# Chunk 0's logits without paired products, short matmuls on ones, a later last store, and a new order of pieces

## The chip, the cores and the metric

The kernel runs on one core of a Trainium2 chip. The metric is the device time of one execution in microseconds; three runs give a median of 217.93 us (217.93 to 218.11).

## What is computed

A layer norm (without weights) of x [2048 x 640] feeds two branches, and the output is x plus both:

```python
def reference(A_x, A_wqkv, A_wo, B_x, B_w1, B_b1, B_w2, B_b2):
    xn = _layernorm(A_x)
    return A_x + _A_ref(xn, A_wqkv, A_wo) + _B_ref(xn, B_w1, B_b1, B_w2, B_b2)
# _A_ref: q, k, v = xn @ wqkv, 32 heads of 20; position s attends to s, s-2, ..., s-14
#         (8 keys, those before 0 masked); softmax; weighted sum of v; @ wo
# _B_ref: gelu(xn @ w1 + b1) @ w2 + b2, width 1536
```

## The kernel before

The 2048 rows are worked off in four chunks (n = 0 to 3) of 512 rows, each of four blocks of 128 rows. One list, ORDER (L38), names small pieces of work; L703 emits them in that order, and every engine, and the DMA queues of SyncE (SP) and ScalarE (ACT), executes its own instructions in the order of emission. GpSimd (POOL) issues the accumulating stores from its queue. A name is a kind, then the chunk, then block or tile:

- `st`, `su`, `sq`, `rs`, `rc`, `xn`: statistics and layer norm. Chunks 0 and 1 take `st` on VectorE (L203; block 1 of chunk 0 on ScalarE), chunks 2 and 3 take `su` and `sq` on ScalarE. `rs` is a square root on ScalarE, `rc` a reciprocal on VectorE.
- `tp`, `tc`: transposition of xn, through TensorE for chunk 0 (copies on VectorE and ScalarE, L279), by DMA from SP for the others (L286).
- `ga`, `gb`, `gd`, `ge` (L331) and `hj<which><pair><columns>` (L362): q, k, v of chunk 0, of one block or of two blocks at a time; `gc` and `hc` empty their PSUM banks on ScalarE. `pj<n><which><tile>` (L318) and `pc` (L377) do that for chunks 1 to 3, in five matmuls of 512 columns each.
- `qk<n><block><half>` (L402): products of q and shifted k on VectorE, eight a chunk, four window steps by five tiles each. `pa` (L420): adds tile 1 to tile 0 and tile 3 to tile 2 of the products, four instructions a chunk, in the chunks named in PAIRED.
- `lg` (L429): sums the products over a head by matmuls with a matrix of zeros and ones. A matmul for every tile, half and block: 3 x 2 x 4 = 24 where products are paired, 5 x 2 x 4 = 40 where not.
- `m`, `mx`, `ex`, `ss`, `ri`, `at`: softmax, on VectorE but for the exponential `ex` on ScalarE. `xd` (SP) and `xs` (ScalarE's queue) copy the attention weights to all rows of a head (L499). `av` (L514), `ad` (L523), `ot` (L528): weighted sum of v on VectorE; `ot` leaves oT.
- `f1<n>_<ft>` (L535): the hidden layer, five matmuls of 512 columns a piece; `ge` with a chunk and a number (L551): bias and GELU on ScalarE. The piece named only `ge` belongs to q.
- `o<n><block><pc>` (L571 the first 512 columns, "lo"; L573 the last 128, "hi"): the output. Parts 0 to 3 take w2, part 4 takes oT and wo. `oc` (L578, L579) empties lo and hi into osb on ScalarE, `od` (L584) adds osb to the output in memory from POOL's queue. `xp`, `xb`: x and the bias b2 go to the output in memory first.
- The last block, 3,3, has its lo in `o330` to `o334`, its hi in `ohi`; `oclo` and `ochi` add x on VectorE (L592, L601) and store without accumulation, `oclo` from SP (L593), `ochi` from ScalarE's queue (L604).
- `tb` and `b1` (L411, L414): transposition of b1 and its copy on VectorE. `ho` builds the matrix for `lg`.

PSUM: psA has four banks, for q, k, v, hidden pieces, transposes and a part of the last chunk's output; psL holds the logits (and the tiles `idle` and `tb`), psO one lo and one hi. osb has two buffers. `table()` (L164) loads ScalarE's function table when sqrt, exp and GELU alternate. Before the list, ten matmuls on ones (L701) run.

Of the kernel before, what the change touches and what calls it, by code (L numbers as in the profile page):

```python
# [13 lines left out]
BF16 = mybir.dt.bfloat16  # L14
F32 = mybir.dt.float32

S, D, F, H, W, DIL = 2048, 640, 1536, 32, 8, 2
P = 128
# [3 lines left out]
CH = 512  # L22
NCH = S // CH
BPC = CH // P
# [5 lines left out]
LASTB = S // P - 1  # L30
WARM = 10

PAIRED = (0, 2, 3)
ACT_STATS = (2, 3)

COLS = ((0, 2), (2, 4), (4, 5))

ORDER = """  # L38
pad01 pad02 st00a st00 sum1 rs00 mean1 neg1 rc00 sq1 xn00a xn00b tp00a tp00b tc00a rs01 tb ga tc00b rc01 xn01 gb2 b1
tp01 gb3 tc01a tc01b gb4 gd gc0 ge st03a st03 rs03 gc1 hj100 st02a rc03 ho hc100 hj101 st02 rs02 hj201 xn03 tp03 rc02  # L40
xn02 st11a st12a st11 st10a gc4 st13a tp02 hc101 tc03 tc02 hc201 hj102 hj200 hc200 hj011 hc102 st10 hc011 st13 st12
rs1 rc1 qk000 qk001 xn12 tc12 hj112 hc112 xn11 qk011 hj010 hc010 tc11 hj111 hj110 hj202 hc202 hc111 qk010 pa010 hj012
hc012 hc110 qk021 qk030 qk031 xn10 qk020 pa011 hj211 hc211 tc10 hj212 f10_11 f10_2 xn13 tc13 hc212 ge0_2 f10_9 ge0_9
f10_0 ge0_0 f10_6 pj114 ldx ld2 pj100 ge0_6 pc100 pj110 pc110 pj102 pad11 pa000 pj112 pa001 lg0 mask m0 ge0_11 pc114
mx0 pc112 pj111 pc102 su22 su20 ex0 ss0 pj103 pj113 pc103 pc111 pc113 pj104 pc104 pj101 pc101 ri0 at0 f10_1 qk110
qk130 f11_9 qk120 su23 f10_10 qk101 ge1_9 su21 f11_10 ge0_10 ge0_1 ng2 f11_3 ge1_3 sq21 f10_4 ge0_4 sq23 f11_0 ge1_0
pj124 pc124 qk121 sq22 f11_7 ge1_7 f10_7 xd0 qk100 qk131 sq20 pj121 ge0_7 rs2 hj210 hc210 qk111 xs0 lg1 ldo rc2 pc121
xn23 av001 tc23 m1 pj123 pc123 av000 xn22 av010 f10_5 av020 av011 mx1 f11_4 o000 ge0_5 ge1_10 xn21 f10_3 ge0_3 tc22
f10_8 av030 ge0_8 xn20 f11_5 ge1_5 o001 o002 o003 tc21 ex1 pj122 av021 xp0 xb0 ss1 pj120 xp1 pc122 tc20 pj211 pc211
xb1 av031 pc120 su32 ri1 ad00 pj204 pc204 at1 xd1 ad01 ad02 ot0 pj203 pad12 av111 pc203 av101 su30 pj222 pc222 pj224  # L50
pc224 pj221 pc221 xs1 av121 pj212 pc212 pj220 pc220 pj223 pj202 pc202 pc223 pj213 pc213 pad22 su33 pj201 f11_1 pc201
su31 av110 pj210 o004 oc00 od00 pj214 av100 pad21 pc214 pc210 ng3 sq31 av130 o020 o021 av131 av120 o022 o023 sq30 sq32
o024 oc02 sq33 rs3 rc3 pj200 pc200 xn31 tc31 o030 o031 o032 o033 o034 xn30 tc30 oc03 ad10 od03 f11_6 o010 o011 o012
ge1_4 xn32 pad31 ad11 tc32 ad12 o013 qk211 xn33 f12_0 o014 f12_4 ge1_1 ge1_6 oc01 od01 ot1 qk221 ge2_0 qk230 qk231
qk220 qk210 ge2_4 qk201 pa211 pa210 f11_2 ge1_2 tc33 pj320 pj304 pc304 qk200 pa201 pj301 pc301 pj324 pj310 pc324 pa200
pj303 pc303 pj323 pc323 pad32 pc320 pj312 pj302 xp2 pc302 pj314 pc314 pc312 xl pj313 pj300 pc313 pj311 f13_6 lg2 pc311
m2 pc310 ge3_6 o130 pc300 qk310 mx2 f11_8 ge1_8 f12_10 o131 o132 qk321 ex2 ss2 ri2 at2 qk301 qk330 qk320 qk331 qk300
f13_11 pa311 f13_5 ge3_5 f13_10 ge3_10 ge2_10 qk311 ge3_11 f13_4 f13_0 xs2 f13_3 ge3_3 pa300 ge3_4 ge3_0 f11_11 ge1_11
f12_8 f12_9 pa301 ge2_8 f13_8 ge3_8 pj322 o133 o134 oc13 od13 pc322 f13_1 ge3_1 pa310 o110 o111 o112 lg3 m3 xd2 av210
xb2 mx3 f12_3 ge2_3 av211 ex3 ss3 f12_7 f13_2 o113 o114 oc11 od11 od02 f13_7 ge3_7 av200 ri3 o100 av230 o101 o102 o103  # L60
xb3 ge3_2 o104 oc10 at3 xs3 f12_6 av231 o120 f12_2 ge2_2 av201 av221 ge2_9 ge2_7 o121 o122 av220 o123 od10 f12_5 ge2_5
f12_11 o124 oc12 od12 ad20 ad21 ad22 ot2 pj321 pc321 av331 xd3 av300 av301 av321 f12_1 ge2_1 av311 ge2_6 f13_9 o210
ge3_9 o211 ge2_11 o212 o213 o310 o214 oc21 od21 o330 o331 o200 o201 o202 o203 o204 oc20 od20 o311 o312 o220 o221 o222
av330 av310 o223 o224 o313 av320 ad30 oc22 od22 ad31 ad32 o230 o231 o232 o233 o234 oc23 od23 o332 o333 o320 o321 o322
o323 ot3 o324 oc32 od32 o314 o300 o334 o301 o302 o303 o304 ohi oc31 od31 oclo ochi oc30 od30
""".split()


# [1 line left out]
def kernel(  # L70
# [16 lines left out]
    nc = tc.nc  # L87
# [3 lines left out]
    out_sd = out.rearrange("b s d -> (b s) d")  # L91
# [5 lines left out]
    psL = ctx.enter_context(tc.tile_pool(name="psL", bufs=1, space=bass.MemoryType.PSUM))  # L97
# [73 lines left out]
    mask = consts.tile([H, W, MW], BF16, name="mask")  # L171
# [20 lines left out]
    tiles = {}  # L192
# [207 lines left out]
    def do_qk(n, j, h):  # L400
# [5 lines left out]
            op=ALU.mult,  # L406
        )

    def do_tb():
        tiles["tb"] = psL.tile([P, 2 * W * P], BF16, tag="L", name="tb")  # L410
        nc.tensor.transpose(tiles["tb"][:, 0:MW], b1_rt[:], ident[0:MW, 0:MW])  # L411
# [10 lines left out]
    def do_lg(n):  # L422
        L = psL.tile([P, W, P], F32, tag="L", name="L")
        tiles["L", n] = L
        ts = range(0, KT, 2 if n in PAIRED else 1)
        for t in ts:
# [160 lines left out]
    last = (NCH - 1, BPC - 1)  # L587
# [11 lines left out]
    def do_ochi():  # L599
        osb = tiles["osb", last]  # L600
        nc.vector.tensor_tensor(  # L601
            out=osb[:, CH:D], in0=tiles["hi", *last][:, 0 : D - CH], in1=x_sb[:, LASTB, CH:D], op=ALU.add
        )
        nc.scalar.dma_start(out_sd[LASTB * P :, CH:D], osb[:, CH:D])  # L604

    pieces = {}

    def piece(name, fn, *args):
        assert name not in pieces
        pieces[name] = lambda: fn(*args)  # L610

    for name in "tb b1 mean1 ho ldx ld2 ldo xl oclo ohi ochi mask".split():
        piece(name, locals()[f"do_{name}"])
    for u, a, b, eng, own in (("a", 0, 2, "ve", "lo"), ("b", 2, KT, "se", "hi")):
        piece(f"xn00{u}", do_xn, 0, 0, a, b)
# [13 lines left out]
            piece(f"tc0{bl}", do_tc, 0, bl, 0, KT, "se")  # L629
    piece("sum1", do_su, 0, 1)  # L630
    piece("neg1", do_ng, 0, 1, 2)
    piece("sq1", do_sq, 0, 1)
    piece("ga", do_ga, 0, 2)
    for ti in range(2, KT):
# [10 lines left out]
    for n in range(NCH):  # L645
# [23 lines left out]
        for h in range(2):  # L669
            for j in range(BPC):  # L670
                piece(f"qk{n}{j}{h}", do_qk, n, j, h)
                piece(f"av{n}{j}{h}", do_av, n, j, h)
            if n in PAIRED:
                for c in range(2):
# [20 lines left out]
    engines = {getattr(mybir.EngineType, e) for e in ("PE", "DVE", "Activation", "SP")}  # L695
    with tc.manual_schedule(engines=engines):

        ones = nc.const_aps.tensor(1.0, [P, CH], BF16)
        idle = psL.tile([P, W, P], F32, tag="L", name="idle")
        for _ in range(WARM):  # L700
            nc.tensor.matmul(idle[:, 0:BPC, :], lhsT=ones[:, 0:P], rhs=ones, start=True, stop=True)  # L701
        assert sorted(ORDER) == sorted(pieces)
        for name in ORDER:  # L703
            pieces[name]()
# [30 lines left out]
```

## Time and profile before

| | us |
|---|---|
| median of three runs | 217.93 |
| the profiled execution | 219.77 |
| its span, first to last instruction | 217.4 |
| TensorE busy | 206.9 |
| VectorE busy | 179.2 |
| ScalarE busy | 125.4 |

The page gives the busy time of each engine as a share of the span; a matmul's row lasts until its result has drained, so rows overlap, and the pace is read from the distance of starts. The chain of waits goes back from the last instruction to what released it. The timeline gives each group of instructions with its start, the idle time in front of it, and what ended that. Times in it are microseconds from the span's start.

### The profile page before, as it was taken

Reading aid. Unit: us, or ns where it says so; the run is one execution under the profiler, and the core shown is the slowest. Engines: PE = TensorE matmul, PEld = TensorE weight load, DVE = VectorE, ACT = ScalarE, POOL = GpSimd, SP = SyncE. Lnnn points to the kernel's source line nnn. Section 1 sums busy time; section 2 is a strip of 40 time slices with the busy share of each in tenths; the row PEclk is TensorE's granted clock in tenths of the full one; section 3 lists DMA queues with packets and bytes.
Section 4 is the critical chain, followed back from the end, with each engine's and each line's share of the span. In section 5 each row is a group of like instructions: output and inputs, shape, how many; then the busy total and the mean of one; then the engine's idle time right before and its main releaser. Section 6 shows DMA issues by size and latency. Waiting matters only on the chain.

```text
span 217.4 us, 3276 instructions
## 1 busy us (share of the span) xinstructions
PE 206.9 (95%) x1327; PEld 115.0 (53%) x1327; DVE 179.2 (82%) x166; ACT 125.4 (58%) x239; POOL 19.7 (9%) x37
## 2 busy tenths in 40 slices
PE   8999989999999998999999999999999999999970
PEld 2899635444645554555555544454555455555540
DVE  3578896599799999998999979996999999994010
ACT  5468595999989747689854558631844520111210
POOL 2000000000000500111010400000110101111301
PEclk9999999999999999999999999999999999999997
DMA  6991249418275996015521491702039202222232
GB/s 217 390 398 56 59 108 386 175 18 233 44 142 166 205 186 182 4 29 90 92 30 71 150 175 29 191 5 30 0 39 207 28 13 33 30 30 33 31 59 31
DMA packets 24069, 23.89 MB, mean 110 GB/s; under 512 B 9080, under 2 KB 21880, under 8 KB 24056
## 3 DMA queue, kind: packets, MB, share of 16 engines
q1 hardware_dynamic: 17008, 14.68, 23.3%
q0 software_dynamic: 4144, 4.92, 17.0%
q10 hardware_dynamic: 2904, 4.10, 5.9%
q8 instruction: 10, 0.16, 0.3%
q14 instruction: 3, 0.02, 0.0%
HBM read 10.00 MB, written 7.54 MB: 81 GB/s over the span
## 4 chain that ended last, share of the span: by engine, by line
PE 64%; DVE 13%; issue 11%; ACT 3%; DMA 3%; POOL 2%; ACTq 1%; POOLq 0%; SPq 0%
PE hps L535 19%; PE lo L571 17%; PE pps L318 15%; DVE half L514 5%; PE hi L573 4%; PE gps L362 3%; PE L L429 3%; DVE half L402 3%; DMA wq_sb<-in_A_wqkv_dram 3%; POOL out_dram L584 2%; PE gps L331 2%; DVE half L523 1%; DVE L L451 1%; DVE m L445 1%; ACTq L499 1%
## 5 line engine op out<-in xcount | busy, mean ns | idle before, releaser
L535 PE MATMUL hps<-xnT,w_sb 128*128 128x512 bf16 x240 | 55.4, 379 | 1.3 <-ACT hT L551 0.9
L402 DVE TENSOR_TENSOR half<-qT,kT 128x2560 bf16<-128x2560 bf16 x32 | 45.8, 1484 | 0.7 <-ACT kT L372 0.7
L571 PE MATMUL lo<-w_sb,hT 128*128 128x512 bf16 x144 | 41.0, 379 | 0.0
L535 PEld LDWEIGHTS <-w_sb 128*128 128x128 bf16 x240 | 22.9, 98 | 28.6 <-issue 2.5
L578 ACT CAST osb<-lo 128x512 bf16<-128x512 f32 x15 | 8.8, 585 | 42.7 <-issue 24.6
L573 PE MATMUL hi<-w_sb,hT 128*128 128x128 bf16 x144 | 31.5, 219 | 0.0
L551 ACT ACTIVATE hT<-hps,b1T 128x512 bf16<-128x512 f32 x36 | 23.5, 685 | 11.5 <-PE hps L535 11.5
L514 DVE TENSOR_TENSOR half<-vT,ax 128x2560 bf16<-128x2560 bf16 x16 | 23.1, 1478 | 1.2 <-PE L L429 1.2
L571 PEld LDWEIGHTS <-hT 128*128 128x128 bf16 x144 | 14.1, 98 | 17.2 <-issue 0.4
L571 PE MATMUL lo<-wo,oT 128*128 128x512 bf16 x80 | 23.1, 379 | 0.0
L584 POOL DMA_DIRECT2D out_dram<-osb x15 | 13.0, 864 | 110.0 <-ACT osb L579 94.1
L514 DVE TENSOR_TENSOR half<-vT,x_sb 128x2560 bf16<-128x2560 bf16 x16 | 22.6, 1483 | 0.0
L523 DVE TENSOR_TENSOR half<-half,half 128x5120 bf16<-128x5120 bf16 x8 | 22.3, 2813 | 0.1
L318 PE MATMUL pps<-xnT,wq_sb 128*128 128x512 bf16 x75 | 18.3, 379 | 1.0 <-ACT kT L377 1.0
L318 PE MATMUL pps<-xnT,wk_sb 128*128 128x512 bf16 x75 | 18.5, 379 | 0.0
L318 PE MATMUL pps<-xnT,wv_sb 128*128 128x512 bf16 x75 | 18.0, 379 | 0.0
L167 ACT ACT_TABLE_LOAD x13 | 16.7, 1283 | 1.0 <-PEq L719 0.7
L573 PE MATMUL hi<-wo,oT 128*128 128x128 bf16 x80 | 16.9, 219 | 0.0
L573 PEld LDWEIGHTS <-hT 128*128 128x128 bf16 x144 | 14.1, 98 | 1.7
L420 DVE TENSOR_TENSOR half<-half 128x2048 bf16<-128x2048 bf16 x12 | 14.1, 1216 | 0.0
L318 PEld LDWEIGHTS <-wq_sb 128*128 128x128 bf16 x75 | 8.7, 117 | 8.7 <-issue 1.6
L377 ACT CAST kT<-pps 128x512 bf16<-128x512 f32 x15 | 8.4, 590 | 7.7 <-PE pps L318 4.8
(86 smaller groups left out, 265.4 us busy)
## 6 DMA issues: line engine op xcount, KB each, us to landing
w_sb<-in_B_w_dram SPq DMA_DIRECT2D x4, 960.0 KB, 11.3
out_dram<-osb POOLq DMA_DIRECT2D x15, 160.0 KB, 3.4
out_dram<-b2bc POOLq DMA_DIRECT2D x3, 640.0 KB, 7.1
x_sb<-in_A_x_dram SPq DMA_DIRECT2D x1, 1280.0 KB, 7.8
out_dram<-x_sb ACTq DMA_DIRECT2D x1, 1120.0 KB, 4.8
ax<-attn SPq DMA_DIRECT2D x4, 256.0 KB, 4.3
ax<-attn ACTq DMA_DIRECT2D x4, 256.0 KB, 5.2
x_sb<-attn SPq DMA_DIRECT2D x4, 256.0 KB, 4.5
```

The source lines that it names most:

```text
L167: nc.scalar.activation(warm[:], nc.const_aps.tensor(0.0, [P, 1], F32), func)
L318: nc.tensor.matmul(ps[:], lhsT=wqkv_p[which][:, ti, to, :], rhs=xnT[:, ti, :], start=(ti == 0), stop=(ti == KT - 1),)
L402: nc.vector.tensor_tensor(out=half[h][:, :, :, cs], in0=qkv_tile(n, 0)[:, :, cs].unsqueeze(1).to_broadcast([P, W // 2, KT, P]), in1=window ...
L420: nc.vector.tensor_tensor(out=even, in0=even, in1=odd, op=ALU.add)
L514: nc.vector.tensor_tensor(out=half[h][:, :, :, cs], in0=window(qkv_tile(n, 2), h, cs), in1=ax_view(n)[:, j, ws, :].unsqueeze(2).to_broadca ...
L523: nc.vector.tensor_tensor(out=a, in0=a, in1=b, op=ALU.add)
L535: nc.tensor.matmul(ps[:], lhsT=w1_sb[:, ti, ft * P : (ft + 1) * P], rhs=tiles["xnT", n][:, ti, :], start=(ti == 0), stop=(ti == KT - 1),)
L551: nc.scalar.activation(hT, tiles["hps", n, ft][:], ACT.Gelu_apprx_tanh, bias=b1T[:, ft : ft + 1], scale=1.0)
L571: nc.tensor.matmul(lo[:], lhsT=lhs, rhs=rhs[:, 0:CH], start=first, stop=last)
L573: nc.tensor.matmul(hi[:, 0 : D - CH], lhsT=lhs, rhs=rhs[:, CH:D], start=first, stop=last)
L578: nc.scalar.copy(osb[:, 0:CH], tiles["lo", n, bl][:])
L584: nc.gpsimd.dma_start(rows, tiles["osb", n, bl][:], accum_op=ALU.add)
```

## The change

Six things:

1. PAIRED loses chunk 0: its four `pa` pieces (pa000, pa001, pa010, pa011) are gone, and lg0 has 40 matmuls instead of 24.
2. A function do_warm issues matmuls on ones into the tile `idle`. Ten of 512 columns come first, as before, then three of 128 columns.
3. Two pieces of such short matmuls stand in the list: `wa` (one) behind tp00a, `wb` (two) behind tp00b.
4. The last store from ScalarE's queue is a piece of its own, `ochd`, the last in the list.
5. The tile `idle` is made before the list is built.
6. ORDER is new throughout. Each engine has the same pieces but for those above, in another order.

```diff
-PAIRED = (0, 2, 3)
+PAIRED = (2, 3)
 ACT_STATS = (2, 3)
...
 ORDER = """
-pad01 pad02 st00a st00 sum1 rs00 mean1 neg1 rc00 sq1 xn00a xn00b tp00a tp00b tc00a rs01 tb ga tc00b rc01 xn01 gb2 b1
-tp01 gb3 tc01a tc01b gb4 gd gc0 ge st03a st03 rs03 gc1 hj100 st02a rc03 ho hc100 hj101 st02 rs02 hj201 xn03 tp03 rc02
-xn02 st11a st12a st11 st10a gc4 st13a tp02 hc101 tc03 tc02 hc201 hj102 hj200 hc200 hj011 hc102 st10 hc011 st13 st12
-rs1 rc1 qk000 qk001 xn12 tc12 hj112 hc112 xn11 qk011 hj010 hc010 tc11 hj111 hj110 hj202 hc202 hc111 qk010 pa010 hj012
-hc012 hc110 qk021 qk030 qk031 xn10 qk020 pa011 hj211 hc211 tc10 hj212 f10_11 f10_2 xn13 tc13 hc212 ge0_2 f10_9 ge0_9
-f10_0 ge0_0 f10_6 pj114 ldx ld2 pj100 ge0_6 pc100 pj110 pc110 pj102 pad11 pa000 pj112 pa001 lg0 mask m0 ge0_11 pc114
...
-o323 ot3 o324 oc32 od32 o314 o300 o334 o301 o302 o303 o304 ohi oc31 od31 oclo ochi oc30 od30
+pad01 pad02 st00a st00 sum1 rs00 mean1 neg1 rc00 sq1 xn00a xn00b tp00a wa tp00b wb tc00a rs01 ga tc00b rc01 xn01 gb2
+tp01 gb3 tc01a tc01b gb4 gd gc0 ge tb b1 ho hj102 st02a gc1 st03a hc102 gc4 st02 rs02 st03 hj100 rs03 rc02 hc100 rc03
+xn02 xn03 hj101 st12a hc101 st11a st13a hj201 st10a tp02 tc02 tp03 hj200 tc03 st11 hc201 hc200 hj202 hc202 hj012 hj110
+hc110 st12 st13 st10 rs1 hc012 qk001 hj010 hc010 hj111 rc1 xn12 qk000 qk011 qk010 xn11 hj011 hc011 tc12 tc11 hj112
+hc111 hc112 f10_1 ge0_1 qk020 xn13 tc13 qk030 f10_11 qk031 f10_6 ge0_6 xn10 f10_0 ge0_0 pad11 f10_9 hj211 hc211 ge0_9
+f10_2 hj212 qk021 lg0 hc212 ge0_11 tc10 pj103 ge0_2 pc103 mask m0 mx0 ex0 ss0 pj114 pj101 pc101 pj104 pc104 pj111
+pj113 pc114 pj112 pj102 pc111 ri0 ldx ld2 su23 pj100 pc113 pj110 at0 su21 pc112 su20 f11_0 pc102 pc100 pc110 qk110
+qk101 qk130 f11_7 qk111 qk131 qk120 qk100 f10_4 xd0 su22 ng2 ge1_7 sq20 f11_3 ge1_3 ge1_0 f10_5 sq22 qk121 pj122 ge0_5
+sq21 ldo ge0_4 hj210 xp0 xs0 f10_3 ge0_3 pj121 sq23 rs2 rc2 o000 o001 lg1 hc210 av010 av000 m1 xn21 f10_7 tc21 pc122
...
+o002 pj120 av020 av021 ex1 ss1 pc120 xp1 av031 ri1 pj124 pc124 o003 av011 pad21 tc23 pj213 pc213 pc123 pj202 pc202
+pj211 pc211 pj214 pc214 at1 pj222 pad12 ge1_10 pc222 pj204 pj224 pc224 xs1 pj200 ad01 ad00 pc200 pj201 su31 ad02 ot0
...
+o312 o230 o231 o232 o233 o234 o313 av311 av331 av320 av301 ad31 ad30 ad32 oc23 ot3 o320 o321 o322 o323 o324 o314 od21
+oc32 od23 o300 o301 o302 o303 o304 oc31 od32 o333 o334 od31 oc30 od30 oclo ohi ochi ochd
 """.split()
...
+    ones = nc.const_aps.tensor(1.0, [P, CH], BF16)
+    idle = psL.tile([P, W, P], F32, tag="L", name="idle")
+
+    def do_warm(n, cols):
+
+        for _ in range(n):
+            nc.tensor.matmul(
+                idle[:].rearrange("p w c -> p (w c)")[:, 0:cols],
+                lhsT=ones[:, 0:P],
+                rhs=ones[:, 0:cols],
+                start=True,
+                stop=True,
+            )
...
-        nc.scalar.dma_start(out_sd[LASTB * P :, CH:D], osb[:, CH:D])
+
+    def do_ochd():
+        nc.scalar.dma_start(out_sd[LASTB * P :, CH:D], tiles["osb", last][:, CH:D])
...
+    piece("wa", do_warm, 1, P)
+    piece("wb", do_warm, 2, P)
...
-        ones = nc.const_aps.tensor(1.0, [P, CH], BF16)
-        idle = psL.tile([P, W, P], F32, tag="L", name="idle")
-        for _ in range(WARM):
-            nc.tensor.matmul(idle[:, 0:BPC, :], lhsT=ones[:, 0:P], rhs=ones, start=True, stop=True)
+        do_warm(WARM, CH)
+        do_warm(3, P)
```

## The prediction

> **What bounds the kernel now.** I read the page first, then the chain that ended last, then the timeline of each engine at the start, at TensorE's gaps and at the end.
>
> ```profile
> PE 206.9 (95%) x1327; PEld 115.0 (53%) x1327; DVE 179.2 (82%) x166; ACT 125.4 (58%) x239; POOL 19.7 (9%) x37
> ```
>
> TensorE is the bound: its rows leave almost no holes from 5.46 us to its last matmul, which starts at 210.52 and ends at 210.58 at the pace of its neighbours. I call that end E. So the end moves only by TensorE's work, its holes, or what follows E.
>
> The timeline of TensorE shows the holes (columns: start, duration, engine, line, operation; a group's duration includes the drain of its last matmul, so I count starts: 0.216 us for 512 columns):
>
> ```profile
> 24.84 1.24 PE L535 MATMUL hps<-xnT,w_sb 128*128 128x512 bf16 x5
> 26.44 3.61 PE L535 MATMUL hps<-xnT,w_sb 128*128 128x512 bf16 x15 [0.36 <-ACT kT L372]
> 30.91 1.24 PE L535 MATMUL hps<-xnT,w_sb 128*128 128x512 bf16 x5 [0.85 <-ACT hT L551]
> ...
> 37.47 1.48 PE L429 MATMUL L<-half,head_of 128*32 128x512 bf16 x24
> ...
> 42.16 2.55 PE L318 MATMUL pps<-xnT,wq_sb 128*128 128x512 bf16 x10
> ```
>
> Five matmuls from 24.84 should hand over at 25.92, not 26.44: 0.52 us lost. Fifteen from 26.44 end at 29.68, not 30.91: 1.23. Ten from 42.16 end at 44.32; the next row starts at 44.54: 0.22. At 82.79 another 1.13 goes (ten matmuls from 79.50 end at 81.66), behind ScalarE, which spent 79.79 to 82.11 issuing chunk 1's two copies of attention weights. Sum 3.10 us, each time for a PSUM bank that ScalarE had not emptied.
>
> The timeline after E shows the tail:
>
> ```profile
> 210.62 0.29 DVE L601 TENSOR_TENSOR osb<-hi,x_sb 128x128 bf16<-128x128 f32 x1 [2.81 <-PE hi L573]
> 210.94 0.35 ACTq L604 DMA_DIRECT2D out_dram<-osb  x1
> 211.41 0.58 ACT L578 CAST osb<-lo 128x512 bf16<-128x512 f32 x1 [6.70 <-DVE osb L601]
> 211.89 0.27 ACT L579 CAST osb<-hi 128x128 bf16<-128x128 f32 x1
> 212.46 0.86 POOL L584 DMA_DIRECT2D out_dram<-osb  x1 [6.59 <-ACT osb L579]
> ```
>
> The copies of block 3,0 (oc30) stand in ScalarE's queue behind the last store, which waits for VectorE, which waits for E. So an accumulating store that could have left earlier is issued at E+1.88, lands 3.36 us later at 215.82, and the program ends 1.60 us after that: E+6.84.
>
> **The tail, new order.** After o304, TensorE still has o333 (3 matmuls of 512 columns, 0.65), o334 (5, 1.08) and ohi (17 of 128, 17 x 0.056 = 0.95). So o304 ends at E-2.7. ScalarE's queue is then empty: oc30 takes 0.15 + 0.75 and its store is issued 0.30 later (as 212.16 to 212.46), at E-1.5; 3.36 to land: E+1.9. The other end, ochi and ochd: 0.39 from E to the issue as now, 1.47 to land (the 32 KB row's): E+1.9. Nothing is queued behind ochd. osb has two buffers: oc30 needs od32's landing, about 0.15 + 0.75 + 0.30 + 3.4 = 4.6 us after o324, while o304 ends 1.36 + 4.62 = 6.0 after it. oclo needs od31's, 6.1 after o324, and its operand comes at 7.7. Both covered. With 1.60 behind the landing: E+3.5, so **-3.35 us**. Bounds: -2.5 if stores side by side take 1 us longer, -3.7 if they land as the quickest (3.3).
>
> **Logits without additions.** The 16 more matmuls are priced by chunk 1's row, 40 in 2.44 us, against 24 in 1.44: **+1.0** on TensorE. VectorE drops four additions at 1.135 apart, 4.54 us, but they count only if lg0 waits for VectorE. lg0 now needs all eight products.
>
> ```profile
> 32.44 3.49 DVE L420 TENSOR_TENSOR half<-half 128x2048 bf16<-128x2048 bf16 x3
> 39.01 0.29 DVE L440 TENSOR_TENSOR L<-L,mask 32x128 f32<-32x128 f32 x1 [3.08 <-PE L L429]
> ...
> 46.61 11.31 DVE L402 TENSOR_TENSOR half<-qT,kT 128x2560 bf16<-128x2560 bf16 x8
> ```
>
> VectorE was done at 35.92 and waited for TensorE. In the new order five wk/wq pieces of chunk 1 no longer stand before lg0.
>
> **The new order up to lg0.** From the first k piece (11.35, taken as unchanged): 115 matmuls of 256 columns x 0.109 = 12.54, 10 transposes x 0.056, tb 0.1, six hidden pieces x 1.08 = 6.48: lg0 at 31.0. One wait is added: tb moves behind ge, so b1 on VectorE waits until about 11.6 (it ran at 6.80). Behind it stand ho and the statistics of blocks 2 and 3, which now start at 9.59. That puts xn02 near 15.2 and costs TensorE's transposes about 0.2. The eight statistics of chunk 1 then end near 19.7 (18.12 now), the first product ends at 21.1, rc1 takes 0.35, seven products x 1.402 end near 31.3: level with lg0. Banks: ScalarE must load the GELU table (1.28 + 0.20) after hc112 (near 24.6); its next outputs follow at 26.8, 28.2 and 29.7, and f10_9, hj211, f10_2 ask for those banks at 27.4, 28.5, 29.5. Only the last waits, 0.25. So the 0.52 and 1.23 go, 0.45 comes, and lg0 starts near 31.5.
>
> **From lg0 on.** Chunk 1's first product needs pj110, the tenth piece behind lg0: 31.5 + 2.44 + 10.8 + 0.65 to evict = 45.4 (VectorE is free at about 41.6, so it idles 3.8). Eight products end at 56.6; TensorE reaches lg1 after 10.8 + 8 x 1.08 + 1.09 + 1.63 at 56.1, against 57.60: 0.2 lost, since lg1's first matmuls need only the first products. ScalarE reaches chunk 1's copies of attention weights (xs1) only after pc224, when they are long ready; I charge 0.25 for its 2.32 us of issuing instead of 1.13. Chunk 2's rc3 will stall VectorE about 3 us (0.59 now), as its statistics stay behind oc02; it has that to spare. From lg3's end to the last oT VectorE now needs 48.2 us (150.25 to 198.49). With lg3 ending near 149 that gives 197.2, and o324 is reached at E-10.1 = 199.3. Covered by 2 us; beyond that each microsecond moves the end. The other moves hide behind TensorE. TensorE's sum: -3.10 + 1.0 + 0.45 + 0.2 + 0.25 = **-1.2**. Bounds: +1.9 if as much is lost as now besides what I added, -2.1 if none of my new waits comes.
>
> **The short matmuls on ones.**
>
> ```profile
> 0.78 4.43 PE L701 MATMUL idle<-const-bfloat16-1.0 128*128 128x512 bf16 x10 [0.78 <-PEq L719]
> 5.46 0.79 PE L274 MATMUL tp<-ident,xn 128*128 128x128 bf16 x5 [0.26 <-DVE xn L259]
> 6.19 0.19 PE L411 MATMUL tb<-ident,b_rt 16*128 16x16 bf16 x1
> 6.72 1.79 PE L331 MATMUL gps<-xnT,wq_sb 128*128 128x128 bf16 x15 [0.35 <-DMA wq_sb<-in_A_wqkv_dram]
> 8.84 2.67 PE L331 MATMUL gps<-xnT,wq_sb 128*128 128x128 bf16 x35
> ```
>
> Starts are 0.427 us apart in the first row and 0.107 from 6.72 to 9.91, half pace; from 10.01 they are 0.056. Three matmuls (0.32) now follow the ten and end at 5.32, before 5.46; one and two more fall into the holes at 5.65 and 6.05. They delay nothing as long as xn00a and wq land no earlier. If full pace came before 6.72, about 30 matmuls would take 0.056 instead of 0.107: -1.5. Bounds 0 and -1.5; I take 0, since the five fill only 0.6 of the 1.1 us idle between 5.0 and 6.72, and 4.2 us of unbroken warm-up had not raised the pace.
>
> The Trainium skill, "TensorE: Matmul & The Clock Gate", section "What's actually happening", says that the gate watches free-running windows of 3413 ns and opens after a busy one. The pace here changes 3.3 us after 6.72, which agrees. By the rule a window from 6.6 back to 3.2 would be fuller, and the change would gain the 1.5. Its section "Part 4: PE-mode transpose" says that transposes do not count as busy, which speaks against it, since they fill part of that window; no row here shows whether they count.
>
> **Sum.** -3.35 - 1.2 + 0 = -4.6 us (rounded): span 217.4 to 212.8. The profiled execution took 219.77, 2.37 around its span; it becomes 215.2. The median of the runs shown is 217.93, 1.84 below; the same step gives **213.3**.
>
> **Rivals.**
> - *Full pace comes early*: another -1.5, 211.8; with few of the new waits, 211.0. For it: the holes are filled by half. Against: ten warm matmuls did not do it. 0.20.
> - *The bank waits come back* (also: the new order does not do what it should): four banks and a ScalarE full from 45 to 55 speak for it, the spacing above against. -3.35 + 1.0 + 0 to 0.9: 215.6 to 216.5. 0.23.
> - *Slower: VectorE decides in the last chunk.* lg3 comes so late that the last oT holds o324. The price is 1:1 beyond 2 us of delay; the time is above 217.93 once lg3 ends 6.6 us later than 149. VectorE's 3.8 + 3 us of new idling speak for it, its idling anyway in front of lg2 and lg3 (1.9 in front of lg3) against. 10 us late: 221. 0.09.
>
> **Chances.** Forecast, 212.3 to 214.6: 0.48. About 0.2% (0.4 us) is what a measurement can tell from no change. Faster 0.88 (0.48 + 0.20 + most of 0.23, cut for the edge), same 0.03, slower 0.09. Range 211.0 to 216.4.
>
> **What would show it.** oc30's copies before ochi; the last store's issue at E+0.4; lg0's 40 matmuls near 31.5; no holes at 24 to 31 and 82; starts at 0.107 until about 9.9. It is wrong if E is above 211, or if VectorE's last oT ends less than 10.1 us before E.

## The result, and the profile after

| | before | after |
|---|---|---|
| median, 4 runs each, us | 218.02 (217.93 to 218.63) | 215.08 (214.75 to 215.61) |
| ratio after/before | | 0.9865 (95%: 0.9843 to 0.9887) |
| the profiled execution, us | 219.77 | 215.14 |
| its span, us | 217.4 | 212.6 |
| E, the end of the last matmul | 210.58 | 209.25 |
| tail, span less E | 6.84 | 3.38 |

The change makes the kernel faster by 1.35%. Against the forecast: 213.3 was predicted (212.3 to 214.6), 215.08 came, above that band and inside the whole range. The span was predicted at 212.8 and measured at 212.6, and still the time is 1.8 us off; the first experiment explains that. The ratios leave out single disturbed executions; one of g2_paired_later, the profiled one, took 270 us. (In the prediction the start of the last matmul of before should read 210.36, not 210.52; E is right.)

The busy times, from the page of the profile after:

```profile
PE 205.3 (97%) x1327; PEld 114.6 (54%) x1349; DVE 174.2 (82%) x162; ACT 126.3 (59%) x241; POOL 19.8 (9%) x37
```

VectorE lost 5.0 us and four instructions, the additions. TensorE's share looks better, but its busy time counts the slow pace of the start too, so the share alone says little. (The counts of PE and PEld differ because some matmul records are missing; a doubled distance between two starts shows where.)

The timeline of all engines at the end (start, duration, engine, line, operation, in brackets the idle time in front and what ended it):

```profile
206.60 0.58 ACT L592 CAST osb<-lo 128x512 bf16<-128x512 f32 x1 [3.87 <-PE hi L587]
...
207.65 0.86 POOL L598 DMA_DIRECT2D out_dram<-osb  x1 [3.76 <-ACT osb L593]
...
209.12 0.36 SPq L607 DMA_DIRECT2D out_dram<-osb  x1
209.29 0.29 DVE L615 TENSOR_TENSOR osb<-hi,x_sb 128x128 bf16<-128x128 f32 x1 [0.20 <-PE hi L587]
209.61 0.36 ACTq L620 DMA_DIRECT2D out_dram<-osb  x1
```

The tail is what lies between E and the end of the span. The copy of block 3,0 now runs 2.65 us before E (before: 0.83 after it), its store is issued 1.6 us before E, and the last store 0.36 us after E with nothing behind it. All three stores land within 0.55 us of each other: POOL's at 211.03, SP's at 211.37, ScalarE's at 211.58.

TensorE from the k, v pieces of chunk 0 to lg0 (L443):

```profile
21.35 2.37 PE L549 MATMUL hps<-xnT,w_sb 128*128 128x512 bf16 x9
25.07 3.60 PE L549 MATMUL hps<-xnT,w_sb 128*128 128x512 bf16 x15 [1.35 <-ACT kT L372]
28.82 1.25 PE L362 MATMUL gps<-xnT,wv_sb 128*128 128x256 bf16 x10
30.21 1.24 PE L549 MATMUL hps<-xnT,w_sb 128*128 128x512 bf16 x5
...
31.92 2.34 PE L443 MATMUL L<-half,head_of 128*32 128x512 bf16 x40
```

Counted by starts as in the prediction: two pieces (ten matmuls, one record missing) from 21.35 should hand over at 23.51, not 25.07: 1.56 us lost. Fifteen from 25.07 end at 28.31, not 28.82: 0.51. Ten of 256 columns from 28.82 end at 29.91, not 30.21: 0.30. So 2.4 us of holes stand where 0.25 was priced. The largest is ScalarE's doing; its row in the waits of the profile after (engine, tile, line, whom it waited for: us in all, times, longest):

```profile
ACT kT L372 <- DVE half L402: 2.0, 1, 2.0
```

and its timeline:

```profile
24.44 0.86 ACT L372 CAST kT<-gps 128x512 bf16<-128x512 f32 x2 [2.01 <-DVE half L402]
25.31 1.28 ACT L167 ACT_TABLE_LOAD   x1
```

hc111, a copy of k, waits for a product of VectorE. The kernel before had such waits too, 2.0 us in two, and I passed over them. These are its copies of k of blocks 2 and 3 (hc112, hc111, hc110):

```profile
20.28 0.35 ACT L372 CAST kT<-gps 128x256 bf16<-128x256 f32 x1
...
23.66 0.58 ACT L372 CAST kT<-gps 128x512 bf16<-128x512 f32 x1 [0.69 <-DVE half L402]
...
25.81 0.58 ACT L372 CAST kT<-gps 128x512 bf16<-128x512 f32 x1 [1.28 <-DVE half L402]
```

In after the wait holds the GELU table load, and so the next banks, until 25.31.

### The profile page after: what moved, and what is told of

The parts are those of the page before. It is cut to its first block, busy times and chain, and to the rows that moved or that the text cites. A ratio compares the mean times of both kernels' runs of the same rounds, so it can differ in the third digit from the quotient of the medians.

```text
span 212.6 us, 3291 instructions
## 1 busy us (share of the span) xinstructions
PE 205.3 (97%) x1327; PEld 114.6 (54%) x1349; DVE 174.2 (82%) x162; ACT 126.3 (59%) x241; POOL 19.8 (9%) x37
## 4 chain that ended last, share of the span: by engine, by line
PE 86%; DVE 8%; ACT 3%; issue 1%; DVEq 0%
PE lo L585 26%; PE pps L318 22%; PE hps L549 19%; DVE half L402 8%; PE hi L587 8%; PE gps L362 4%; PE L L443 3%; PE idle L415 2%; PE gps L331 1%; ACT hT L565 1%; ACT xn L257 1%; PE tp L274 1%; ACT L167 1%; ACT kT L372 0%; ACT kT L377 0%
## 5 line engine op out<-in xcount | busy, mean ns | idle before, releaser
L402 DVE TENSOR_TENSOR half<-qT,kT 128x2560 bf16<-128x2560 bf16 x32 | 45.8, 1486 | 5.3 <-ACT kT L377 3.6
L585 PE MATMUL lo<-w_sb,hT 128*128 128x512 bf16 x136 | 39.7, 379 | 0.1
L587 PE MATMUL hi<-w_sb,hT 128*128 128x128 bf16 x144 | 31.5, 219 | 0.5 <-issue 0.2
L585 PE MATMUL lo<-wo,oT 128*128 128x512 bf16 x76 | 22.4, 379 | 0.0
L537 DVE TENSOR_TENSOR half<-half,half 128x5120 bf16<-128x5120 bf16 x8 | 22.2, 2820 | 0.1
L318 PE MATMUL pps<-xnT,wk_sb 128*128 128x512 bf16 x75 | 18.0, 379 | 0.1
L318 PE MATMUL pps<-xnT,wq_sb 128*128 128x512 bf16 x72 | 17.4, 379 | 0.1
L585 PEld LDWEIGHTS <-oT 128*128 128x128 bf16 x80 | 7.8, 98 | 9.4
L318 PEld LDWEIGHTS <-wk_sb 128*128 128x128 bf16 x75 | 8.7, 118 | 7.3
```

Of the source, the lines that this page charges most:

```text
L318: nc.tensor.matmul(ps[:], lhsT=wqkv_p[which][:, ti, to, :], rhs=xnT[:, ti, :], start=(ti == 0), stop=(ti == KT - 1),)
L402: nc.vector.tensor_tensor(out=half[h][:, :, :, cs], in0=qkv_tile(n, 0)[:, :, cs].unsqueeze(1).to_broadcast([P, W // 2, KT, P]), in1=window ...
L537: nc.vector.tensor_tensor(out=a, in0=a, in1=b, op=ALU.add)
L585: nc.tensor.matmul(lo[:], lhsT=lhs, rhs=rhs[:, 0:CH], start=first, stop=last)
L587: nc.tensor.matmul(hi[:, 0 : D - CH], lhsT=lhs, rhs=rhs[:, CH:D], start=first, stop=last)
```

## The experiments

Two theories at first. **Mine after the result:** the whole gain is the tail; the rest of the new order gains nothing, and the drop of E in the two profiles (1.33 us) comes from the pace at which TensorE ran its first matmuls in the one execution that the prediction read. **Rivals:** the order gains about 1.2 us as forecast and the tail less than forecast; or the short matmuls on ones bring an early full pace.

**e1_before.** The kernel before, unchanged, to see other executions of it.

> The kernel before, unchanged, with the span of every run. Question: the changed kernel's profiled span fell as forecast (217.4 to 212.6) but the measured medians only by 2.9 us, from 218.0 to 215.1. Theory 'late pace': in the profiled execution TensorE reached its full pace at 10.0 us, later than it mostly does; most runs have it 1.5 to 1.8 us of work earlier, so most spans lie near 215.6, the profiled one at 217.4 was a late one, and a new profile shows starts 0.056 us apart well before 9.9. Rival 'around the span': spans are near 217.4 in every run, and the runs differ from the profiled execution in what lies around the span.

Measured: 218.0 against 217.99, ratio 0.9995 (0.9963 to 1.0027); span 215.3 in the profiled execution. The timeline of TensorE at its start:

```profile
6.15 1.05 PE L331 MATMUL gps<-xnT,wq_sb 128*128 128x128 bf16 x15
...
7.31 2.12 PE L331 MATMUL gps<-xnT,wq_sb 128*128 128x128 bf16 x35
9.27 2.35 PE L362 MATMUL gps<-xnT,wk_sb 128*128 128x256 bf16 x20
```

The same fifteen matmuls that took 1.79 us in the profile of the prediction take 1.05 here: full pace (starts 0.056 apart) is granted from 6.25 us, not from 9.99. The first k piece starts at 9.27 instead of 11.35, and E is 208.75 instead of 210.58. (Of these 2.08 us, 0.57 lie ahead of the fifteen matmuls, which start at 6.15 and not at 6.72; there they had waited 0.35 for wq.) Of the 35 runs of this kernel beside this experiment, 29 spans lie between 215.3 and 216.5, and six between 216.7 and 218.8. So the profile that the prediction was made from belonged to a late execution: the 1.84 us between it and the median were TensorE's start, and the same amount could not be subtracted again from an execution of after that started earlier (full pace from 6.80).

**e2_tail.** Before, with the tail alone.

```diff
-o323 ot3 o324 oc32 od32 o314 o300 o334 o301 o302 o303 o304 ohi oc31 od31 oclo ochi oc30 od30
+o323 ot3 o324 oc32 od32 o314 o300 o301 o302 o303 o304 oc31 od31 oc30 od30 o333 o334 oclo ohi ochi ochd
```

(o333 is taken from ahead of o320, ochd is a piece of its own.)

> The kernel before with the tail of the change alone: oc30 and its store ahead of ochi, the last store a piece of its own, o333 and o334 behind o304. Theory: -3.35 us as worked out in the prediction (end of the span at E+3.5 instead of E+6.84), whatever the pace at the start does. Rival 'stores collide': the last three stores now land side by side and each takes about 1 us longer, -2.4. Rival 'order paid it back': the tail is worth 3.35, and the rest of the change then lost about 0.4 of the 2.9 that were measured.

Measured: 215.18 against 217.99, ratio 0.986 (0.9826 to 0.9894): 2.8 us, less than the 3.35 expected, and nearly as much as the whole change (2.9). The timeline of its end:

```profile
207.42 0.86 POOL L584 DMA_DIRECT2D out_dram<-osb  x1 [3.76 <-ACT osb L579]
...
209.39 0.35 ACTq L606 DMA_DIRECT2D out_dram<-osb  x1
```

E is 209.03, the tail 3.51 us, against 6.58 in e1_before: 3.07 shorter, while E itself comes 0.28 later.

**e3_short.** Before, with the six short matmuls alone (three behind the ten, `wa`, `wb`).

> The kernel before with the short matmuls on ones alone (three behind the ten, one behind tp00a, two behind tp00b). Theory 'late pace': TensorE reaches full pace near 6.8 us in the profile, the early pieces are done 1.6 us sooner, but most runs of the kernel before already have that, so the median moves by 0 to -0.5 us. Rival 'pace pays in full': -1.5 us in the median. Rival 'no effect': full pace at 9.9 as before, 0.

Measured: 218.02 against 217.99, ratio 1.000 (0.9979 to 1.0021). In its profiled execution full pace came at 4.82, but the spans of its runs (215.3 to 216.8) cover the same stretch as most of before's. **e4_noshort** is the counterpart, after without them:

```diff
-... tp00a wa tp00b wb tc00a ...
+... tp00a tp00b tc00a ...
...
-        do_warm(3, P)
```

> The changed kernel without the six short matmuls, everything else as changed. Theory 'late pace': median between 0 and +0.5 us above the changed kernel (215.1 to 215.6), with single runs up to 1.6 us longer where the pace comes late. Rival 'pace pays in full': +1.5 us, 216.6.

Measured: 214.7 against 217.99, ratio 0.9856 (0.9812 to 0.99); after itself gave 214.73 in f1_after, below. The medians show no effect of the short matmuls. Its profiled execution (span 214.9) was a late one: wq landed late, TensorE idled 1.23 us in front of 7.14, and the pace was full from 4.18 to 7.6, half to 11.0, then full again:

```profile
7.14 1.44 PE L331 MATMUL gps<-xnT,wq_sb 128*128 128x128 bf16 x15 [1.23 <-DMA wq_sb<-in_A_wqkv_dram]
...
8.90 3.13 PE L331 MATMUL gps<-xnT,wq_sb 128*128 128x128 bf16 x35
```

35 matmuls in 3.13 us here, 2.12 in e1_before. It is the same spread again: the first k piece starts at 12.07 here and at 9.43 in f1_after.

**f1_after.** After, unchanged, beside the runs that follow.

> The changed kernel again, to stand beside the others of this call: 215.1 us, all theories.

Measured: 214.73 against 218.18, ratio 0.9839 (0.9816 to 0.9863); span 212.1, E 208.84, full pace from 4.45.

Next, the hole behind hc111. hc111 writes k of blocks 2 and 3 in two of the five tiles, 2 and 3. The products ahead of it in the list (qk000, qk011, qk010) read k of blocks 0 and 1 in all five tiles (L402). They share no element, yet the copy waits. My first guess was the negative step in the window of the product, which could make its extent look larger than it is.

**f2_window.** After, with the window's step turned round and the mask's index with it.

```diff
-        first = PAD - DIL * (W // 2 * h) + cs.start
+        first = DIL * (W // 2 * h) + cs.start
...
-            ap=[[part, n_part], [-DIL, W // 2], [tile_step, n_tile], [1, n_col]],
+            ap=[[part, n_part], [DIL, W // 2], [tile_step, n_tile], [1, n_col]],
```

> The changed kernel with the eight key positions of a window counted upwards instead of downwards (positive step in the window's access pattern, the mask laid out to match; the sums are the same). Observation: in the changed kernel ScalarE's copies of the second k pair (hc111, hc112) wait until VectorE's products of block 1 (qk011, qk010) are done, 24.4 us, though these read no column that the copies write; TensorE then has a hole of 1.5 us at 23.3 and of 0.3 at 28.3 and 29.8. Theory 'false overlap': the waits come from the negative step, which makes the products seem to reach six columns further; with a positive step the wait on VectorE goes, the holes with it, -1.5 to -2.0 us, 213.3. Rival 'banks and table': the holes come from four banks and the loading of the GELU table, and little changes, 0 to -0.4 us.

Measured: 214.76 against 218.18, ratio 0.9841 (0.9816 to 0.9866), and the row in its waits is the same as in after:

```profile
ACT kT L372 <- DVE half L402: 2.0, 1, 2.0
```

That guess fell.

**f3_paired.** After, with chunk 0 paired again, its four additions directly ahead of lg0. **f4_unpaired.** Before, with chunk 0 unpaired alone.

```diff
-PAIRED = (2, 3)
+PAIRED = (0, 2, 3)
...
-f10_2 hj212 qk021 lg0 hc212 ...
+f10_2 hj212 qk021 pa010 pa011 pa000 pa001 lg0 hc212 ...
```

> The changed kernel with chunk 0's products paired again, the four additions directly ahead of lg0, nothing else moved. Theory: VectorE is done with chunk 0's products at 31.0 and lg0 starts at 31.9, so the additions (4.54 us) make lg0 wait 3.6 us, the 16 matmuls saved give 1.0 back, and since chunk 1's products wait for pj110 behind lg0, all of it stays: +2.6 us, 217.7. Rival 'covered': VectorE idles 3.6 us in front of chunk 1's products, so the additions are taken from there and only the matmuls count: -1.0 us.

> The kernel before with chunk 0's products unpaired alone (the four additions left out, 40 matmuls instead of 24 in lg0), order, tail and start as before. Theory: VectorE waited 3.1 us for lg0 and gains nothing, TensorE gets 1.0 us more: 218.9. Rival 'VectorE earlier': the 4.5 us that VectorE saves let TensorE's later waits shrink, -0.5 or better.

Measured: f3_paired 218.87 against 218.18, ratio 1.0021 (0.9995 to 1.0048), 4.1 us over after; 2.6 were expected. f4_unpaired 218.82 against 218.18, ratio 1.0017 (0.9996 to 1.0039): 0.64 more between the medians, which the interval does not tell from zero, against 1.0 by the count of matmuls. TensorE in f3_paired:

```profile
34.81 0.39 PE L443 MATMUL L<-half,head_of 128*32 128x512 bf16 x2 [2.49 <-DVE half L434]
35.94 2.58 PE L443 MATMUL L<-half,head_of 128*32 128x512 bf16 x22 [0.74 <-DVE half L434]
```

lg0 waits 2.49 and 0.74 us for the additions, and then a second cost follows that I did not expect. Between 36.16 and 39.30 the matmuls of lg0 (in groups of four) and the first single ones behind them start 0.42 to 0.43 apart, twice the 0.216 of full pace; the granted clock is half from 36.15 to 39.56. Of these 3.41 us half, 1.7, is lost in this execution, after 3.41 us that were mostly idle. That the idling caused it is read from this one profile. In f4_unpaired VectorE's waits have this row, which stood at 3.1 in before:

```profile
DVE L L440 <- PE L L429: 7.7, 1, 7.7
```

All that VectorE saves with the additions (4.5 us) turns into waiting for TensorE, and lg0's row grows from 1.41 us to 2.28 (36.48 to 38.76 here). Dropping them pays only where the order brings lg0 forward, as the new one does: there paired products would hold TensorE. In the old place it costs the 16 matmuls.

**g1_copy_early.** After, with hc111 (and its matmuls, hj111) issued ahead of the products that it waited for.

```diff
-... hc012 qk001 hj010 hc010 hj111 rc1 xn12 qk000 qk011 qk010 ... tc12 tc11 hj112
-hc111 hc112 f10_1 ...
+... hc012 qk001 hj111 hj010 hc010 rc1 hc111 xn12 qk000 qk011 qk010 ... tc12 tc11 hj112
+hc112 f10_1 ...
```

> The changed kernel with one pair of pieces moved: hj111 ahead of hj010, and its copy hc111 ahead of qk000, qk011 and qk010 instead of behind them. Counting the window upwards left ScalarE's wait on VectorE as it was, so the step's sign is not its cause. Theory 'overlap across tiles': a product reads its window in all five tiles, and hc111 writes tiles 2 and 3, between the first and the last element that the product reads, so it has to wait for the products issued ahead of it though no column is shared; issued ahead of them it does not wait. Then the wait of 2.0 us goes, the GELU table is loaded 1.5 to 1.9 us earlier, TensorE's hole of 1.5 us at 23 goes with the smaller ones behind it: -1.5 to -2.0 us against the changed kernel, 213.0. Rival 'banks and table': the hole stays, 0 to -0.3 us.

Measured: 213.66 against 218.01, ratio 0.9789 (0.9761 to 0.9816), the fastest version; 1.1 to 1.4 us under after, where 1.5 to 2.0 were expected. ScalarE's timeline:

```profile
22.73 0.39 ACT L372 CAST kT<-gps 128x256 bf16<-128x256 f32 x1
23.14 1.28 ACT L167 ACT_TABLE_LOAD   x1
```

and TensorE's:

```profile
21.11 5.56 PE L549 MATMUL hps<-xnT,w_sb 128*128 128x512 bf16 x25
...
30.74 2.12 PE L443 MATMUL L<-half,head_of 128*32 128x512 bf16 x34 [0.38 <-DVE half L402]
```

The 2.0 us wait is gone, the table is loaded at 23.14 instead of 25.31, 25 matmuls of the hidden layer run without a hole, and lg0 starts at 29.75; there it waits 0.38 us for VectorE's last product, the next bound. By starts, lg0 takes 3.04 us (29.75 to 32.79) and not 2.28 as in after: 0.76 of the gain is given back there. One detail speaks for the cause: hc112 writes the last tile alone, and it stays behind the same three products. VectorE ran these until about 25.0 (its row of products starts at 20.78, about 1.42 apart), and hc112 ran at 22.73 without waiting. A range from the first to the last element that the products read takes in columns of blocks 2 and 3 in every tile but the last. So what is waited for fits the extent of the operand, not the elements in it. The three rows of before fit as well: hc112 ran at 20.28, with qk000 and qk001 ahead of it until about 22.2 (three products from 19.34, 1.4 apart), while hc111 and hc110, which write tiles 2 and 3 and tiles 0 and 1, each waited for the end of the product ahead. That the extent decides is inferred from these copies; what the run shows is that the wait hangs on the order of issue.

**g2_paired_later** and **h2_paired_later_again** are one kernel: g1_copy_early with chunk 0 paired, and lg0 put behind four more pieces of chunk 1, so that the additions should be hidden. The loads ldx and ld2 and the copies pc111, pc113 and pc114 also move forward, ex0 and ss0 back.

```diff
-PAIRED = (2, 3)
+PAIRED = (0, 2, 3)
...
-f10_2 hj212 qk021 lg0 hc212 ge0_11 tc10 pj103 ge0_2 pc103 mask m0 mx0 ex0 ss0 pj114 pj101 pc101 pj104 pc104 pj111
-pj113 pc114 pj112 pj102 pc111 ri0 ldx ld2 su23 pj100 pc113 pj110 at0 ...
+f10_2 hj212 qk021 pa010 pa011 pa000 pa001 hc212 ge0_11 tc10 ldx ld2 pj103 ge0_2 pc103 pj114 pc114 pj101 pc101 pj104 pc104 lg0 mask m0 mx0 pj111
+pj113 pc111 pc113 ex0 ss0 pj112 pj102 ri0 su23 pj100 pj110 at0 ...
```

> As the run before (hc111 early), with chunk 0's products paired again and lg0 moved behind four of chunk 1's projections (pj103, pj114, pj101, pj104), so that VectorE's additions run while TensorE has other work. Theory: VectorE's additions take the time that it idled in front of chunk 1's products, TensorE saves the 16 matmuls: another -0.6 to -1.0 us, 212.2. Rival 'ScalarE': exp and the projections' copies crowd each other and the softmax of chunk 0 comes later, 0 to +1 us.

> The version with hc111 early, paired products and lg0 behind four projections once more, for a profile that can be read: its median was 1.9 us above the version without pairing, where -0.6 to -1.0 was expected. Theory 'lg0 late': the profile shows TensorE or VectorE waiting around lg0 and lg1 for 1.5 us or more longer than without pairing. Rival 'banks': TensorE waits for banks behind the projections that stand close together ahead of lg0.

Measured: 215.57 against 218.01, ratio 0.9883 (0.984 to 0.9925), and again 215.15 against 218.13, ratio 0.9869 (0.985 to 0.9889): 1.5 to 1.9 us slower than g1_copy_early, where 0.6 to 1.0 faster was expected. TensorE in the second:

```profile
31.46 1.25 PE L318 MATMUL pps<-xnT,wq_sb 128*128 128x512 bf16 x5 [1.00 <-ACT hT L565]
...
44.84 4.60 PE L549 MATMUL hps<-xnT,w_sb 128*128 128x512 bf16 x20 [0.83 <-ACT kT L377]
50.07 1.24 PE L549 MATMUL hps<-xnT,w_sb 128*128 128x512 bf16 x5 [0.63 <-ACT hT L565]
```

lg0's 16 matmuls are saved and it starts at 35.87, as the additions end, but three holes of 0.6 to 1.0 us come, each for a bank that ScalarE had not emptied. So ScalarE's queue, not VectorE's, makes this version slow. What part is due to pairing and what to the moved pieces was not separated.

**h1_old_tail.** After, with the old order of the tail: the new order, the unpaired products and the short matmuls are left.

```diff
-... ot3 o320 o321 o322 o323 o324 o314 od21 oc32 od23 o300 o301 o302 o303 o304 oc31 od32 o333 o334 od31 oc30 od30 oclo ohi ochi ochd
+... ot3 o333 o320 o321 o322 o323 o324 od21 oc32 od23 od32 o314 o300 o334 o301 o302 o303 o304 ohi oc31 od31 oclo ochi ochd oc30 od30
```

> The changed kernel with the tail of before: o333 ahead of block 2's output, o334 ahead of o301, and the last store ahead of oc30 in ScalarE's queue; order, unpaired logits and short matmuls as changed. Theory 'tail is the gain': the tail alone gave -2.8 us on the kernel before; taken away here it costs as much, and what is left of the change is -0.2 to -0.7 us against before: 217.3 to 217.8. Rival 'the order is the gain too': 216.6 or less, with -1.2 us left as the prediction summed it.

Measured: 218.27 against 218.13, ratio 1.0015 (1.0002 to 1.0029). Nothing of the gain is left, not even the 0.2 to 0.7 us that were expected. The timeline of its end:

```profile
209.61 0.36 ACTq L620 DMA_DIRECT2D out_dram<-osb  x1
210.09 0.58 ACT L592 CAST osb<-lo 128x512 bf16<-128x512 f32 x1 [6.70 <-DVE osb L615]
...
211.13 0.86 POOL L598 DMA_DIRECT2D out_dram<-osb  x1 [6.60 <-ACT osb L593]
```

The copy stands behind the last store again, with the same 6.70 us of idling as in before, and the tail is 6.56.

## Why the prediction was right, and where it was wrong

**The tail, -3.35: right in its steps, 2.8 to 3.5 in size.** Alone it brings 2.8 us in the median (e2_tail); taken out of after it costs 3.2 to 3.5 (218.27 against 215.08 and 214.73). Step by step: the store of block 3,0 was issued at E-1.6 (E-1.5 predicted) and took 3.38 to land (3.36). The last store was issued at E+0.36 (0.39), and landed 1.97 us later, not 1.47; SP's took 2.3 instead of 1.7. So three stores side by side do cost half a microsecond, the pessimistic bound had asked for a whole one. That was given back at the end: 1.05 us from the last landing to the end of the span, not 1.60. In all E+3.38 against E+3.5. The 1.60 was no constant: it is 1.59 to 1.60 in the five profiles in which POOL's store lands last, and 0.91 to 1.07 in the eight in which ScalarE's does.

**The short matmuls, 0: right in the medians,** by e3_short and e4_noshort. What I argued with ("4.2 us of unbroken warm-up had not raised the pace") was one execution, though. In e1_before the same warm-up was followed by full pace at 6.25, and over all profiled executions it first came between 3.4 and 6.80 us with the short matmuls and between 4.18 and 9.99 without.

The traces also record the granted clock, and it changes only at multiples of 3.41 us. An estimate from the rows, each matmul counted as its spacing at half pace (0.427 us for 512 columns, 0.107 for 128), gives TensorE's busy share in each stretch of 3.41 us. Stretches after which the pace stayed at half were at most 76.4% busy (before 68%, up to 6.58 us; after 76.4%, up to 3.39). Those that brought full pace were at least 76.9% busy (h1_old_tail 76.9%, up to 3.40; e1_before 80.8%, up to 6.25). The six short matmuls, 0.64 us, would have lifted the 68% of the prediction's execution to about 87%. So they can matter where the phase is unlucky; whether they make late executions rarer was not shown. The shares count the transposes. Without them e1_before's stretch would be about 66% busy, less than the 76.4% that did not suffice in after, so here transposes seem to count, which the prediction left open.

**TensorE's sum, -1.2: this is the step that failed.** E did fall by 1.33 in the two profiles, but the pace at the start gave more than that. Counted from the first k piece, where every execution used here has reached full pace, to E:

| kernel | first k piece | E | between |
|---|---|---|---|
| before (the prediction's profile) | 11.35 | 210.58 | 199.23 |
| e1_before | 9.27 | 208.75 | 199.48 |
| e3_short | 9.37 | 208.54 | 199.17 |
| e2_tail | 9.28 | 209.03 | 199.75 |
| after | 9.84 | 209.25 | 199.41 |
| f1_after | 9.43 | 208.84 | 199.41 |
| h1_old_tail | 9.85 | 209.25 | 199.40 |
| g1_copy_early | 9.60 | 207.95 | 198.35 |

With the old tail the new order and lg0 together change +0.1 (199.40 against 199.17 to 199.48), with the new tail -0.3 (199.41 against the one profile of e2_tail), not -1.2. h1_old_tail says the same in medians, 218.27 against 218.13. Of its terms, the holes before lg0 failed (part of -3.10, with the 0.25 priced for new ones); the others came out within 0.3:

- *Holes before lg0.* 0.52 and 1.23 went, and 1.56, 0.51 and 0.30 came, where one wait of 0.25 was priced. From the first k piece to lg0 it took 22.08 us and not 20.15 (31.5 less 11.35). That is 1.93 more; from lg0 to E it was 0.55 less than priced (177.33 against 177.88), which leaves the 1.4 between 198.03 (199.23 less 1.2) and 199.41. That lg0 starts at 31.92, so near the predicted 31.5, is chance: the first k piece came 1.51 us earlier, by the pace, and paid for the holes. The prediction set the GELU table "after hc112 (near 24.6)" and asked for the banks only from 27.4 on; it did not ask what hc111 itself waits for. By its own sum the three products ahead of hc111 end near 25.65 (21.1 + 0.35 + 3 x 1.402), a microsecond later. g1_copy_early takes that one wait away: from the first k piece to lg0 it needs 20.15 us, the predicted figure, and to E 198.35, 1.1 less than after and near the -1.2 of the forecast.
- *lg0, +1.0:* the row has 40 matmuls in 2.28 us from start to next start, in after and in f4_unpaired, against 24 in 1.41 in before (37.47 to 38.88): 0.87. f4_unpaired gives +0.64 between the medians, with an interval of -0.1 to +0.85 (its ratio times 218.18). Right in kind, and 0.1 too large by the rows.
- *xs1:* the hole of 1.13 near 82 is gone as forecast; matmuls run from 76.06 to 85.77 without one. The 0.25 charged there did not show. The 0.2 at lg1 came as 0.36 (its row lasts 2.86 us, 2.50 in before). With the 0.13 that lg0 cost less, these explain 0.2 of the 0.55 by which the stretch from lg0 to E came out better; the rest is not placed.
- *From lg0 on:* chunk 1's products start at 45.84 (45.4 predicted) after 3.56 us of waiting (3.8), in VectorE's timeline of after:

```profile
45.84 11.31 DVE L402 TENSOR_TENSOR half<-qT,kT 128x2560 bf16<-128x2560 bf16 x8 [3.56 <-ACT kT L377]
```

  lg1 follows at 56.47 (56.1). The last oT ends at 197.16 (197.2), so VectorE's cover held and the rival *slower, VectorE decides in the last chunk* did not come. A stall of about 3 us on rc3 does not show in the waits.

**From the profile to the median: the second half of the same error.** I had a profiled execution 1.84 us above its median and subtracted 1.84 at the end, as if it were a constant. It was a property of that execution, and after's profiled execution did not have it: 215.14 against a median of 215.08. With the sum at +0.1 and the tail at -2.8 to -3.3 the forecast from the median, 217.93, would have been 214.7 to 215.2.

**The rivals.** *The bank waits come back* (215.6 to 216.5) was nearest, though 215.08 lies between its band and the forecast's: the holes did move rather than go, through hc111's wait on VectorE, which it did not name. *Full pace comes early* did come, at 6.80 in the profiled execution of after, but also in e1_before and, by their spans, in most executions of before, so it changes no median.

The Trainium skill, "TensorE: Matmul & The Clock Gate", section "What's actually happening", says that the window is free-running and that the cold start varies from run to run by its phase. The runs agree that it varies: the same kernel before was at full pace from 6.25 us in one execution and from 9.99 in another, with 1.83 us between their E. The size differs: the section gives 500 ns either way, and these two lie 3.74 us apart. The prediction quoted the window and overlooked what its phase does to a single profile.

## What to carry to other kernels

Before a sum is made on one profiled execution, compare that execution with the median, and find where the difference sits; if it lies in the first microseconds, make the sum from a point behind it and apply it to the median. A queue that ends with copies waiting behind the last store is worth reordering: here it was the gain to within 0.5 us. Where a wait for a bank goes, look at what the engine that empties the bank waits for itself; a small row in its waits (2.0 us here) becomes the hole of the new order, and issuing the copy ahead of the reader removed it.

## What the runs showed of the hardware that was not expected

- TensorE's pace changes on a grid of 3.41 us, whose phase differs between executions. In e4_noshort full pace lasted from 4.18 to 7.6 and half pace from 7.6 to 11.0; in f3_paired half pace lasted from 36.15 to 39.56. The start of full pace lay between 3.4 and 9.99 us. By the estimate above it came after a stretch at least 76.9% busy; counted in the same way with the spacing at full pace, it was kept after stretches at least 40% busy (h2_paired_later_again, from 208.9) and lost after stretches at most 33% busy (e4_noshort, 4.18 to 7.6).
- A short idle stretch in mid-kernel can cost more than itself: in f3_paired TensorE idled 2.49 and 0.74 us around 32 to 36, so that the stretch from 32.74 to 36.15 was 13% busy (estimated likewise), and then ran 3.41 us at half pace, about 1.7 us of work.
- Three stores side by side land later than spread out: in the eight profiles with the new tail the 32 KB from ScalarE's queue took 1.94 to 2.09 us and SP's 128 KB 2.25 to 2.43; in the five with the old tail 1.47 to 1.48 and 1.71 to 1.72.
- A copy waited for a product that shares no element with it, where the product's operand spans its columns (hc111, 2.0 us), and one into the last tile did not (hc112, in before and in g1_copy_early). Whether the chip needs such a wait or only the program asks for it, no run shows.
